# Attention and a quadratic ReLU FFN on one core: turned attention weights moved in one set of transfers for two head groups, and a planner with other costs, priorities and places

## The chip, the core and the metric

The kernel runs on one core of a Trainium2 chip. The metric is the device time of one execution in microseconds (us). TensorE (PE) multiplies, VectorE (DVE), ScalarE (ACT) and GpSimd (POOL) work on the results, and SyncE (SP) and GpSimd issue most of the transfers. TensorE has two clock levels, 1.2 and 2.4 GHz; the profile gives the granted clock as a share of the full one.

## What is computed

Attention runs inside chunks of 64 rows; its output, with the heads side by side, goes through a feed-forward network with a piecewise quadratic curve.

```python
# q, k, v: 8 x 8 x 576 x 64 (batch, heads, rows, head size), chunk = 64
scores = scale * np.matmul(q_c, k_c.transpose(0, 1, 2, 4, 3))
attn = np.exp(scores - max); attn = attn / (attn.sum(-1) + 1e-09)
out = np.matmul(attn, v_c)
x = out.transpose(0, 2, 1, 3).reshape(4608, 512)
h = x @ w_in                      # 512 x 2048
g = np.where(h >= 1, h, np.where(h <= -1, 0.0, (h + 1) ** 2 / 4))
y = g @ w_out                     # 2048 x 512
```

## The kernel before

**Tiles and groups.** The 4,608 tokens are 9 tiles of 512. A tile has 4 head groups of two heads each. The hidden width of 2,048 is 16 blocks of 128, so a tile has 16 steps of `ffn_in` (12 products of 512 columns) and 16 of `ffn_out` (12 products). Each number is carried as a high and a low part, hence three products for one.

**Stages.** Tiles 0 to 2 go step by step: `ffn_in(t, j)`, two steps later `ffn_out(t, j)`. Tiles 3 to 8 go in pairs (t, t+1). For a pair, `ffn_quad(t, m)` makes two hidden blocks of both tiles at a time with seven mixed products instead of eight (8 quads a pair). It finishes the blocks of tile t at once and sends those of tile t+1 to DRAM (`hold`). Then `recall(t+1, j)` reads them back, so that 16 steps of pure `ffn_out` follow. The mixed weights are made during tiles 1 and 2 by `mix_weights(m)` and written to DRAM (`to_mixed`), from where `load_mixed` reads them. The mixed inputs of a pair are made by `mix_x(t)` with 22 subtractions on VectorE and 14 casts on ScalarE.

**Attention between the steps.** From tile 2 on two head groups go together. `turn_next` transposes q and k of the next two groups into `qT` and `kT` (VectorE, L430). `burst` then makes the values of two groups and the scores of the next two on TensorE, the softmax (VectorE and ScalarE), and the turning back: VectorE transposes the weights in blocks of 32 x 32 into `qT` (L571), which is free by then, and transfers inside SBUF put the blocks in place in `aT` (L560). Behind that stand the loads of v for these groups and of q and k for the ones after them. Bursts stand at steps 4 and 10 of tile 1, at steps 0, 4, 8 and 12 of tile 2, and at quads 0, 2, 4 and 6 of the pairs 3 and 5 (`QUADS`). `turn_next` comes two steps before a burst, or just before the quad that the burst follows. The next `turn_next` writes q into the same `qT` buffers that the transfers of L560 read.

**Order.** Every operation is added to a `Plan` with an engine, a cost, and what it reads and writes. `Plan.emit` then simulates all engines and writes each engine's instructions in the simulated order. Among the parts that are ready on an engine, the one that was added first goes first. On the chip an engine takes its instructions in exactly this order. For a transfer the plan counts issuing (`cost`, split over `sends`), moving, and a `lag` until the data can be used:

```python
for _ in range(sends):
    end = max(end, landed[-self.UNDER_WAY]) + cost / sends
    moved = max(end, moved) + moving / sends
    landed.append(moved + lag)
```

The start order is written out: the loads of tile 0, then `load_more(6)` weights, q and k of tile 1, two more weights, v, four more weights.

Of the kernel before, what the change touches and what calls it, by code (L numbers as in the profile page):

```python
# [18 lines left out]
class Plan:  # L19
# [10 lines left out]
    def __init__(self):  # L30
        self.parts = []
        self.writer = {}
        self.readers = {}
        self.written = {}

    def add(
# [11 lines left out]
        for k in writes:  # L48
            self.written.setdefault(k, []).append(n)
        self.parts.append((engine, cost, emit, needs, lag, columns, port, moving, sends))  # L50
# [17 lines left out]
    def emit(self, filler):  # L68
# [32 lines left out]
        for _ in range(len(parts)):  # L101
            while True:
                best = None
                for e in engines:
                    while soon[e] and soon[e][0][0] <= free[e]:
                        heapq.heappush(now[e], heapq.heappop(soon[e])[1])
# [14 lines left out]
            while soon[e] and soon[e][0][0] <= start:  # L121
                heapq.heappush(now[e], heapq.heappop(soon[e])[1])
            n = heapq.heappop(now[e])
# [29 lines left out]
def kernel(  # L153
# [57 lines left out]
    qT_bufs, kT_bufs = buffers(sb, "qT", 2), buffers(sb, "kT", 2)  # L211
    e_bufs, aT_bufs = buffers(sb, "e", 1), buffers(sb, "aT", 2)
# [29 lines left out]
    words = {}  # L242
    weight = {}
# [40 lines left out]
    def load_weight(w, j):  # L284
# [12 lines left out]
        plan.add("sp", 0.57, emit, (), (f"{w}{j}_0", f"{w}{j}_1"), lag=2.1, moving=1.4)  # L297
# [95 lines left out]
    def load_heads(t, g, which="qkv"):  # L393
        for n, src, bufs in (("q", q, q_bufs), ("k", k, k_bufs), ("v", v, v_bufs)):
# [5 lines left out]
            if BATCH[t] is None or (n, t) == ("v", TURNED):  # L400
# [6 lines left out]
                (), (key,), lag=2.1, moving=1.3 if load == load_blocks else 1.2,  # L407
# [140 lines left out]
    def attn_turn_back(t, g):  # L548
# [3 lines left out]
        def move():  # L552


            src = x.rearrange("p (c e q) -> p c e q", e=2, q=Q)
            dst = aT.rearrange("p (c e q) -> p c e q", e=2, q=Q)
# [7 lines left out]
        if t < FLIPPED:  # L564
            pkey, ps = o_banks[1] if t == 0 else a_banks[0]
            plan.add("pe", 0.45, lambda: flip(ps, e), (ekey,), (pkey,), columns=T)
            plan.add("act", 0.48, lambda: nc.scalar.copy(out=aT, in_=ps), (pkey,), (akey,),
                     lag=late(t, 1.2))
        else:
# [163 lines left out]
    def mix_weights(m):  # L733
# [8 lines left out]
        def whole(n, dst):  # L742
            w = weight["wi", n].bitcast(F32)
            return nc.gpsimd.tensor_tensor(out=dst, in0=w[:, 0, :], in1=w[:, 1, :], op=ALU.add)

        def sum_of(out, x, y, op):
            return lambda: nc.gpsimd.tensor_tensor(out=out, in0=x, in1=y, op=op)
# [362 lines left out]
```

## Time and profile before

| | |
|---|---|
| Median of 3 runs (lowest, highest) | 858.1 us (855.43, 858.96) |
| The profiled execution | 859.44 us, span 857.7 us |
| PE busy | 827.9 us, 97% of the span |
| DVE busy | 554.5 us, 65% |
| ACT busy | 419.8 us, 49% |
| POOL busy | 202.4 us, 24% |
| Mean granted TensorE clock | 0.991 |

The span runs from the first to the last instruction on the engines. Busy TensorE time is a modelled figure, since products overlap; the waits of TensorE are a better measure of what is lost.

### The profile page before, as it was taken

The page shows a single profiled execution, that of the slowest core. Times are in us where ns is not written, and L with a number is a line of the kernel's source. Part 1 is how long each engine was busy: PE and PEld are TensorE (multiplying, and loading weights), DVE is VectorE, ACT ScalarE, POOL GpSimd, SP SyncE. Part 2 cuts the span into 40 slices and gives each one's busy share as a digit, 9 for nine tenths or more (in the row PEclk, how much of TensorE's full clock was granted, in tenths as well). Part 3 has the DMA queues.
Part 4 walks back from the last instruction along what each step waited for, and adds up shares of the span by engine and source line. Part 5 has one row for each costly group of instructions (what it writes and reads, how often), then busy time and mean ns, then how long its engine had stood idle before and what let it go on. Part 6 is the DMA issues. An engine that isn't in the chain of part 4 may idle for free.

```text
span 857.7 us, 15616 instructions
## 1 busy us (share of the span) xinstructions
PE 827.9 (97%) x5766; PEld 678.8 (79%) x5766; DVE 554.5 (65%) x921; ACT 419.8 (49%) x719; POOL 202.4 (24%) x326
## 2 busy tenths in 40 slices
PE   9799989999989999998999999899998999999998
PEld 8587867888878888786877888788886888888886
DVE  5788997757568778774769538577674255454422
ACT  5878864444445455443457224545563245444422
POOL 2221133365565201111112211211212112121210
PEclk9999999999999999999999999999999999999999
DMA  9878785663786656888697716975645254443432
GB/s 203 282 232 282 232 221 134 156 131 98 174 218 131 138 97 170 217 208 191 178 229 214 203 50 206 213 185 173 195 147 166 68 194 162 160 149 122 147 99 75
DMA packets 284828, 146.81 MB, mean 171 GB/s; under 512 B 249296, under 2 KB 257744, under 8 KB 284752
## 3 DMA queue, kind: packets, MB, share of 16 engines
q1 hardware_dynamic: 257728, 61.26, 32.5%
q0 software_dynamic: 24768, 83.90, 30.0%
q10 hardware_dynamic: 2256, 0.66, 0.4%
q8 instruction: 46, 0.75, 0.4%
q14 instruction: 30, 0.25, 0.1%
HBM read 101.71 MB, written 36.70 MB: 161 GB/s over the span
## 4 chain that ended last, share of the span: by engine, by line
PE 75%; DVE 6%; SPq 6%; DMA 5%; issue 5%; ACT 1%; POOL 1%; ACTq 0%; DVEq 0%; POOLq 0%
PE ps_o L670 38%; PE ps_h L847 20%; PE ps_h L635 12%; SPq L560 3%; PE ps_h L470 2%; PE ps_a L452 2%; DMA aT<-qT 2%; DMA words_wo<-in_moe_w_out_dram 1%; PE ps_a L670 1%; DMA q_sb<-in_q_dram 1%; SPq L387 1%; DMA k_sb<-in_k_dram 1%; DMA r<-held 1%; SPq L349 0%; DVE mx L526 0%
## 5 line engine op out<-in xcount | busy, mean ns | idle before, releaser
L670 PE MATMUL ps_o<-parts_wo,gh 128*128 128x512 f32 x1120 | 350.0, 394 | 3.8 <-DVE tmp L694 2.6
L670 PEld LDWEIGHTS ps_o<-parts_wo,gh 128*128 128x128 f32 x1120 | 209.4, 189 | 50.5 <-DVE tmp L694 4.1
L670 PE MATMUL ps_o<-parts_wo,gl 128*128 128x512 f32 x560 | 219.2, 391 | 1.2 <-DVE gl L656 1.2
L847 PE MATMUL ps_h<-big_wi,big_wi 128*128 128x512 f32 x720 | 174.8, 392 | 9.3 <-DVE big_wi L856 6.1
L847 PEld LDWEIGHTS ps_h<-big_wi,big_wi 128*128 128x128 f32 x720 | 135.1, 188 | 39.6 <-DVE big_wi L856 7.6
L656 DVE TENSOR_TENSOR gl<-r,gh 128x512 fp32r<-128x512 f32 x120 | 89.0, 742 | 72.1 <-ACT gh L655 68.0
L655 ACT CAST gh<-r 128x512 fp32r<-128x512 f32 x120 | 74.1, 618 | 119.5 <-PE ps_o L670 55.0
L635 PE MATMUL ps_h<-xh,parts_wi 128*128 128x512 f32 x376 | 125.1, 395 | 6.3 <-DVE r L646 3.7
L670 PEld LDWEIGHTS ps_o<-parts_wo,gl 128*128 128x128 f32 x560 | 105.7, 189 | 24.8 <-DVE gl L656 2.7
L778 POOL DMA_DIRECT2D big_wi<-mixed x84 | 45.1, 537 | 296.0 <-PE ps_h L847 288.7
L635 PEld LDWEIGHTS ps_h<-xh,parts_wi 128*128 128x128 f32 x376 | 70.6, 188 | 23.1 <-DVE r L646 4.6
L635 PE MATMUL ps_h<-xl,parts_wi 128*128 128x512 f32 x188 | 73.5, 391 | 0.0
L861 ACT ACTIVATE tmp<-big_wi 128x512 f32<-128x512 f32 x48 | 30.3, 632 | 73.1 <-DVE big_wi L856 65.8
L847 PE MATMUL ps_h<-xh,big_wi 128*128 128x512 f32 x192 | 63.3, 389 | 0.0
L642 ACT ACTIVATE r<-ps_h 128x512 f32<-128x512 f32 x47 | 27.8, 594 | 44.8 <-PE ps_h L635 44.5
L871 POOL DMA_DIRECT2D held<-tmp x48 | 26.5, 552 | 82.2 <-DVE tmp L865 76.3
L646 DVE SCALAR_TENSOR_TENSOR r<-ps_h,r 128x512 f32<-128x512 f32 x47 | 31.8, 677 | 19.8 <-ACT r L645 19.7
L430 DVE STREAM_TRANSPOSE qT<-q_sb 128x512 f32<-128x512 f32 x32 | 22.5, 705 | 33.3 <-DMA aT<-qT 20.8
L656 DVE TENSOR_TENSOR gl<-big_wi,gh 128x512 fp32r<-128x512 f32 x24 | 16.6, 690 | 40.2 <-ACT gh L655 40.1
L847 PEld LDWEIGHTS ps_h<-xh,big_wi 128*128 128x128 f32 x192 | 36.0, 188 | 7.5
L865 DVE SCALAR_TENSOR_TENSOR tmp<-big_wi,tmp 128x512 f32<-128x512 f32 x48 | 33.1, 690 | 13.5 <-ACT tmp L864 13.4
L635 PEld LDWEIGHTS ps_h<-xl,parts_wi 128*128 128x128 f32 x188 | 35.4, 189 | 7.1
(144 smaller groups left out, 1071.9 us busy)
## 6 DMA issues: line engine op xcount, KB each, us to landing
big_wi<-mixed POOLq DMA_DIRECT2D x84, 512.0 KB, 4.2
held<-tmp POOLq DMA_DIRECT2D x48, 256.0 KB, 3.9
words_wi<-in_moe_w_in_dram SPq DMA_DIRECT2D x16, 512.0 KB, 6.6
words_wo<-in_moe_w_out_dram SPq DMA_DIRECT2D x16, 512.0 KB, 8.2
out_dram<-tmp SPq DMA_DIRECT2D x31, 256.0 KB, 2.9
aT<-qT SPq DMA_DIRECT2D x224, 32.0 KB, 2.5
v_sb<-in_v_dram SPq DMA_DIRECT2D x52, 128.0 KB, 3.5
mixed<-parts_wi POOLq DMA_DIRECT2D x24, 256.0 KB, 3.8
```

The lines of the kernel that those rows point to most:

```text
L560: nc.sync.dma_start(out=dst[b:b + Q, :, i // 2, :], in_=src[a:a + Q, :, i % 2, :])
L635: nc.tensor.matmul(out=ps, lhsT=weight["wi", j][:, half, kc * P:(kc + 1) * P], rhs=x, start=(kc == 0 and i == 0), stop=(kc == KC - 1 and i ...
L642: plan.add("act", 0.48, lambda: nc.scalar.activation(out=r, in_=ps, func=AF.Relu, bias=0.5, scale=0.5), (pkey,), (rkey,))
L646: plan.add("dve", 0.6, lambda: nc.vector.scalar_tensor_tensor(out=r, in0=ps, scalar=1.0, in1=r, op0=ALU.max, op1=ALU.min), (pkey,), (rkey,))
L655: plan.add("act", 0.52, lambda: nc.scalar.copy(out=gh, in_=r), (rkey,), (ghkey,))
L656: plan.add("dve", 0.6, lambda: nc.vector.tensor_tensor(out=gl, in0=r, in1=gh.bitcast(F32), op=ALU.subtract), (rkey, ghkey), (glkey,), port ...
L670: nc.tensor.matmul(out=acc, lhsT=x[:, cols], rhs=weight["wo", j][:, half, :], start=(j == 0 and i == 0), stop=(j == NF - 1 and i == 2),)
L778: plan.add("pool", 0.65, lambda: nc.gpsimd.dma_start(out=place_of(f"wi{slot}").bitcast(F32), in_=mixed[u]), keys, (f"wi{slot}_0", f"wi{slo ...
L847: nc.tensor.matmul(out=bank, lhsT=w[:, c:c + P], rhs=x()[:, kc, :], start=start and kc == 0 and k == 0, stop=kc == 1 and k == 2, skip_grou ...
L861: plan.add("act", 0.5, lambda: nc.scalar.activation(out=r, in_=h(), func=AF.Relu, bias=0.5, scale=0.5), (hkey,), (rkey,))
L865: plan.add("dve", 0.6, lambda: nc.vector.scalar_tensor_tensor(out=r, in0=h(), scalar=1.0, in1=r, op0=ALU.max, op1=ALU.min), (hkey,), (rkey,))
L871: plan.add("pool", 0.65, lambda: nc.gpsimd.dma_start(out=held[j], in_=r), (rkey,), (f"held{j}",), lag=2.1, moving=0.8)
```

## The change

- One tile holds both `qT` buffers and one both `aT` buffers, side by side. `attn_turn_back_pair` transposes the weights of two groups and then moves both with one set of 8 transfers, each twice as large; before, each group had its own 8.
- The plan counts 5.4 us of issuing, 0.8 of moving and 4.9 of lag for that set, where it counted 4.8, 0.4 and 1.7 for a group. Loads of q, k and v for tile 3 and later get a lag of 4.1 instead of 2.1. The first six weight loads count 1.9 us of moving instead of 1.4.
- A part can be added with `plan.behind`: it is ranked as if it had been added that many parts later. `mix_x` is added so with 60 when it stands among the recalled steps.
- The six sums and differences of `mix_weights` run on VectorE instead of GpSimd, and the calls of `mix_weights` stand at other steps.
- Bursts of the pairs 3 and 5 stand at quads 0, 2 and 5 and at step 2 of the recalled tile, instead of quads 0, 2, 4 and 6.
- `load_more` at the start goes 4, 2, 6 instead of 6, 2, 4.

```diff
@@ Plan.add / Plan.emit
+        self.rank.append((n + self.behind, n))
...
-                        heapq.heappush(now[e], heapq.heappop(soon[e])[1])
+                        heapq.heappush(now[e], self.rank[heapq.heappop(soon[e])[1]])
...
-            n = heapq.heappop(now[e])
+            n = heapq.heappop(now[e])[1]
@@ buffers
-    qT_bufs, kT_bufs = buffers(sb, "qT", 2), buffers(sb, "kT", 2)
-    e_bufs, aT_bufs = buffers(sb, "e", 1), buffers(sb, "aT", 2)
+    qT_both, aT_both = (sb.tile([P, 2, T], F32, name=f"{n}_both") for n in ("qT", "aT"))
+    qT_bufs, aT_bufs = (
+        [(f"{n}{i}", both[:, i, :]) for i in range(2)] for n, both in (("qT", qT_both), ("aT", aT_both))
+    )
+    kT_bufs, e_bufs = buffers(sb, "kT", 2), buffers(sb, "e", 1)
@@ load_weight
-        plan.add("sp", 0.57, emit, (), (f"{w}{j}_0", f"{w}{j}_1"), lag=2.1, moving=1.4)
+        plan.add("sp", 0.57, emit, (), (f"{w}{j}_0", f"{w}{j}_1"), lag=2.1,
+                 moving=1.9 if len(asked) < 6 else 1.4)
+        asked.append((w, j))
@@ load_heads
-                (), (key,), lag=2.1, moving=1.3 if load == load_blocks else 1.2,
+                (), (key,), lag=2.1 if t < 3 else 4.1, moving=1.3 if load == load_blocks else 1.2,
@@ attn_turn_back (t >= FLIPPED), now attn_turn_back_pair
+        xkeys, akeys = ([f"{n}{i}" for i in range(2)] for n in ("qT", "aT"))
         def move():
-            src = x.rearrange("p (c e q) -> p c e q", e=2, q=Q)
-            dst = aT.rearrange("p (c e q) -> p c e q", e=2, q=Q)
+            src, dst = (x.rearrange("p g (c e q) -> p (g c) e q", e=2, q=Q) for x in (qT_both, aT_both))
             for j in range(2):
                 for i in range(4):
...
-            xkey, x = room("x", qT_bufs, t, g)
-            plan.add("dve", 0.6, lambda: nc.vector.transpose(out=x, in_=e), (ekey,), (xkey,))
-            plan.add("sp", 4.8, move, (xkey,), (akey,), lag=1.7, moving=0.4, sends=8)
+        for t, g in some:
+            ekey, e = e_room(t, g)
             xkey, x = room("x", qT_bufs, t, g)
+            plan.add("dve", 0.6, lambda x=x, e=e: nc.vector.transpose(out=x, in_=e), (ekey,), (xkey,))
+        plan.add("sp", 5.4, move, xkeys, akeys, lag=4.9, moving=0.8, sends=8)
@@ mix_weights
-            return nc.gpsimd.tensor_tensor(out=dst, in0=w[:, 0, :], in1=w[:, 1, :], op=ALU.add)
+            return nc.vector.tensor_tensor(out=dst, in0=w[:, 0, :], in1=w[:, 1, :], op=ALU.add)
...
-        plan.add("pool", 1.05, lambda: whole(i, a), keys[i], (akey,), port=True)
-        plan.add("pool", 0.6, sum_of(c[:, one], b[:, one], b[:, two], ALU.add), (bkey,), (ckey,), port=True)
+        plan.add("dve", 0.6, lambda: whole(i, a), keys[i], (akey,), port=True)
+        plan.add("dve", 0.35, sum_of(c[:, one], b[:, one], b[:, two], ALU.add), (bkey,), (ckey,), port=True)
...
@@ the order
-    load_more(6)
+    load_more(4)
     load_heads(1, 0, "qk")
     load_more(2)
     load_heads(1, 0, "v")
-    load_more(4)
+    load_more(6)
...
-    QUADS, LATE, MIX_X = (0, 2, 4, 6), -9, 3
-    MIX_AT = {18: (0,), 21: (1,), 24: (2,), 27: (3,), 30: (4,), 33: (5,), 36: (6,), 39: (7,)}
+    QUADS, LATE, MIX_X = (0, 2, 5), 2, 3
+    MIX_AT = {17: (0,), 21: (1,), 25: (2,), 29: (3,), 33: (4,), 37: (5,), 41: (6,), 45: (7,)}
...
-        for at in then:
-            attn_turn_back(*at)
+        if then:
+            attn_turn_back_pair(then)
...
             if j == MIX_X and t + 2 < NTILE:
+                plan.behind = 60
                 mix_x(t + 2)
+                plan.behind = 0
```

## Rows read from the trace of the kernel before

**Rows 1.** The waits of TensorE, asked for the stretches 0 to 60, 60 to 132, 132 to 324, 324 to 474, 474 to 646 and 646 to 858 us, in this order. Columns: who waited on which tile and line, for whom; us in total, times, the longest.

```profile
PE ps_h L635 <- DVE r L646: 3.4, 1, 3.4
...
PE ps_h L635 <- DVE parts_wi L332: 1.4, 2, 1.0
PE ps_o L670 <- DVE gl L656: 1.2, 1, 1.2
PE ps_h L635 <- ACT parts_wi L328: 1.2, 2, 0.9
PE ps_o L670 <- DVE parts_wo L332: 0.7, 1, 0.7
...
PE ps_h L470 <- DVE r L646: 2.2, 1, 2.2
...
PE ps_h L847 <- DVE big_wi L856: 6.1, 3, 3.0
PE ps_o L670 <- DVE tmp L694: 0.8, 1, 0.8
PE ps_h L847 <- DVE r L865: 0.7, 1, 0.7
...
PE ps_h L847 <- DVE r L865: 2.5, 1, 2.5
...
PE ps_o L670 <- DVE tmp L694: 1.8, 1, 1.8
```

**Rows 2.** First a piece of the chain that ended last (start, length, what), then two stretches of the table of stretches: length, busy time of PE, PEld, DVE, ACT and POOL with their instructions, the granted clock, the DMA share, GB/s.

```profile
474.27 35.36 PE ps_o L670 x156
...
398.00:401.20 3.20, 3.20 (x9) 2.46 (x10) 0.00 (x0) 0.00 (x0) 0.46 (x2) 0.56 0.94 277
38.00:43.20 5.20, 4.73 (x14) 3.80 (x15) 5.20 (x10) 4.32 (x8) 0.28 (x1) 0.69 0.73 219
```

**Rows 3.** SyncE's queue in order of time, at three bursts: the start of a run of issues, its length, what is issued, how many.

```profile
239.68 11.00 SPq L560 DMA_DIRECT2D aT<-qT  x16
...
349.36 11.79 SPq L560 DMA_DIRECT2D aT<-qT  x16
...
386.99 10.94 SPq L560 DMA_DIRECT2D aT<-qT  x16
```

**Rows 4.** VectorE in order of time, at the third of these bursts: start, length, instruction, and in brackets the idle time before it with what ended it.

```profile
395.37 0.71 DVE L430 STREAM_TRANSPOSE qT<-q_sb 128x512 f32<-128x512 f32 x1 [5.15 <-DMA aT<-qT]
...
401.88 0.71 DVE L430 STREAM_TRANSPOSE qT<-q_sb 128x512 f32<-128x512 f32 x1 [4.02 <-issue]
```

**Rows 5.** The same view at three other bursts.

```profile
249.81 0.71 DVE L430 STREAM_TRANSPOSE qT<-q_sb 128x512 f32<-128x512 f32 x1 [4.23 <-DMA aT<-qT]
...
358.32 0.71 DVE L430 STREAM_TRANSPOSE qT<-q_sb 128x512 f32<-128x512 f32 x1 [1.87 <-DMA aT<-qT]
...
548.50 0.71 DVE L430 STREAM_TRANSPOSE qT<-q_sb 128x512 f32<-128x512 f32 x1 [5.28 <-DMA q_sb<-in_q_dram]
```

**Rows 6.** First the issues of two lines (ns of one issue: least, median, most; first and last start), then the same transfers in the table of DMA issues (count, KB each, median us from issue to landing).

```profile
L560 SPq DMA_DIRECT2D aT<-qT x224: 585/609/1732, 139.5 to 608.3; - x112
...
L370 SPq DMA_DIRECT2D q_sb<-in_q_dram x96: 338/487/1594, 111.4 to 552.0; - x96
...
aT<-qT SPq DMA_DIRECT2D x224, 32.0 KB, 2.5
...
q_sb<-in_q_dram SPq DMA_DIRECT2D x96, 64.0 KB, 2.9
```

**Rows 7.** Around the turn from a pair's quads to its recalled tile: two pieces of the chain (a burst), VectorE in order of time (the first and the last instruction of a softmax with its turning, and two evictions), and the stretch of the recalled steps in the table of stretches.

```profile
410.60 0.88 PE ps_h L470 x55
...
411.53 0.95 PE ps_a L452 x56
...
446.95 1.29 DVE L526 TENSOR_REDUCE mx<-ps_a 128x8 f32<-128x512 f32 x2 [1.02 <-PE ps_a L452]
...
452.80 1.29 DVE L571 STREAM_TRANSPOSE qT<-kT 128x512 f32<-128x512 f32 x2
...
471.19 0.69 DVE L694 COPY tmp<-ps_o 128x512 f32<-128x512 f32 x1
...
474.00:510.00 36.00, 36.00 (x161) 29.81 (x160) 14.40 (x23) 8.63 (x14) 6.44 (x12) 1.00 0.52 127
...
647.10 0.69 DVE L694 COPY tmp<-ps_o 128x512 f32<-128x512 f32 x1 [1.58 <-DMA held<-tmp]
```

**Rows 8.** The sums of mixed weights on GpSimd (ns least, median, most), VectorE's group of half width (busy us, mean ns), a wait of GpSimd, and two VectorE instructions in order of time.

```profile
L744 POOL TENSOR_TENSOR e<-parts_wi x8: 1277/1290/1305, 117.5 to 270.4; 128x512 f32<-128x512 f32 x8
...
L619 DVE TENSOR_TENSOR xl<-ps_h,xh 128x256 fp32r<-128x256 f32 x2 | 0.8, 415 | 0.0
...
POOL e L744 <- DMA mixed<-e: 4.5, 4, 1.7
...
117.78 1.54 DVE L332 TENSOR_TENSOR parts_wi<-tmp,parts_wi 128x512 fp32r<-128x512 f32 x1
...
126.21 1.22 DVE L656 TENSOR_TENSOR gl<-r,gh 128x512 fp32r<-128x512 f32 x1
```

**Rows 9.** The start: SyncE's queue and VectorE in order of time.

```profile
23.51 11.14 SPq L362 DMA_DIRECT2D q_sb<-in_q_dram  x8
...
37.13 0.71 DVE L430 STREAM_TRANSPOSE qT<-q_sb 128x512 f32<-128x512 f32 x1 [1.65 <-DMA k_sb<-in_k_dram]
```

More of the change, by code (lines that the diff above doesn't have):

```diff
@@ L34, in __init__ @@
         self.written = {}
+        self.behind = 0
+        self.rank = []
     def add(
@@ L121, in emit @@
             while soon[e] and soon[e][0][0] <= start:
-                heapq.heappush(now[e], heapq.heappop(soon[e])[1])
-            n = heapq.heappop(now[e])
+                heapq.heappush(now[e], self.rank[heapq.heappop(soon[e])[1]])
+            n = heapq.heappop(now[e])[1]
             _, cost, emit, _, lag, columns, port, moving, sends = parts[n]
@@ L242 @@
     words = {}
+    asked = []
     weight = {}
@@ L550, in attn_turn_back, with attn_turn_back_pair @@
         akey, aT = room("aT", aT_bufs, t, g)
+        if t < FLIPPED:
+            pkey, ps = o_banks[1] if t == 0 else a_banks[0]
+            plan.add("pe", 0.45, lambda: flip(ps, e), (ekey,), (pkey,), columns=T)
+            plan.add("act", 0.48, lambda: nc.scalar.copy(out=aT, in_=ps), (pkey,), (akey,),
+                     lag=late(t, 1.2))
+    def attn_turn_back_pair(some):
+        xkeys, akeys = ([f"{n}{i}" for i in range(2)] for n in ("qT", "aT"))
         def move():
-            src = x.rearrange("p (c e q) -> p c e q", e=2, q=Q)
-            dst = aT.rearrange("p (c e q) -> p c e q", e=2, q=Q)
+            src, dst = (x.rearrange("p g (c e q) -> p (g c) e q", e=2, q=Q) for x in (qT_both, aT_both))
             for j in range(2):
@@ L743, in whole @@
             w = weight["wi", n].bitcast(F32)
-            return nc.gpsimd.tensor_tensor(out=dst, in0=w[:, 0, :], in1=w[:, 1, :], op=ALU.add)
+            return nc.vector.tensor_tensor(out=dst, in0=w[:, 0, :], in1=w[:, 1, :], op=ALU.add)
         def sum_of(out, x, y, op):
-            return lambda: nc.gpsimd.tensor_tensor(out=out, in0=x, in1=y, op=op)
+            return lambda: nc.vector.tensor_tensor(out=out, in0=x, in1=y, op=op)
         one, two = slice(0, HALF), slice(HALF, T)
-        plan.add("pool", 1.05, lambda: whole(i, a), keys[i], (akey,), port=True)
-        plan.add("pool", 1.05, lambda: whole(j, b), keys[j], (bkey,), port=True)
-        plan.add("pool", 0.6, sum_of(c[:, one], b[:, one], b[:, two], ALU.add), (bkey,), (ckey,), port=True)
-        plan.add("pool", 0.6, sum_of(c[:, two], c[:, one], a[:, one], ALU.subtract), (akey,), (ckey,), port=True)
-        plan.add("pool", 0.6, sum_of(b[:, one], a[:, one], b[:, one], ALU.subtract), (akey,), (bkey,), port=True)
-        plan.add("pool", 0.6, sum_of(b[:, two], a[:, two], c[:, two], ALU.subtract), (akey, ckey), (bkey,), port=True)
+        plan.add("dve", 0.6, lambda: whole(i, a), keys[i], (akey,), port=True)
+        plan.add("dve", 0.6, lambda: whole(j, b), keys[j], (bkey,), port=True)
+        plan.add("dve", 0.35, sum_of(c[:, one], b[:, one], b[:, two], ALU.add), (bkey,), (ckey,), port=True)
+        plan.add("dve", 0.35, sum_of(c[:, two], c[:, one], a[:, one], ALU.subtract), (akey,), (ckey,), port=True)
+        plan.add("dve", 0.35, sum_of(b[:, one], a[:, one], b[:, one], ALU.subtract), (akey,), (bkey,), port=True)
+        plan.add("dve", 0.35, sum_of(b[:, two], a[:, two], c[:, two], ALU.subtract), (akey, ckey), (bkey,), port=True)
         for skey, s_, which in ((ckey, c, (5, 6)), (bkey, b, (7, 3))):
```

6 lines of the change are left out of this document (removed).

## The prediction, made before the change was run

> **What bounds the kernel now.** I read the waits of TensorE first, stretch by stretch [rows 1], because TensorE's busy share says little here: its products are pipelined and overlap in the records. Where nothing waits, 156 products of 512 columns, 13 output steps of 12, follow each other in 35.36 us, 226.7 ns each, at the full clock (the first row of [rows 2]). A shorter time can therefore come only out of the waits, and out of the half-clock stretches behind the long ones. The rows of [rows 1] sum to 22.0 us in 15 waits, 1.47 us each. Behind the 3.0 us wait the granted clock was 0.56 of full speed for 3.2 us, behind the 3.4 us wait 0.69 for 5.2 us (the other rows of [rows 2]); at full being 2.4 GHz and half 1.2 GHz, these lose 3.2 x 0.44 = 1.4 us and 5.2 x 0.31 = 1.6 us. So 25 us is all that any reordering can return; the rest is work that the change leaves alone.
>
> Next I asked who is late. In the quad stages TensorE waits for a VectorE sum (L856) or curve (L865), but those are short; VectorE itself stood still before them. [rows 4] show it standing 5.15 us and then 4.02 us in front of a transposition of q (L430). What holds that instruction is in [rows 3]: the turned attention weights lie in the q buffers, and 16 transfers out of them occupy SyncE's queue from 386.99 for 10.94 us; the first q buffer came free at 395.37, the second at 401.88. The same instruction holds VectorE at three more places [rows 5]: 249.81 and 358.32 (behind the set that begins at 349.36), both for the transfer out of qT, and 548.50 for a load of q which stands on SyncE behind such a set. VectorE takes its instructions in the order that the planner wrote, so everything behind the transposition waits as well, the sums that TensorE needs among it.
>
> The planner put the transposition there because it believed the transfers quicker than they are. It counts 4.8 us of issuing, 0.05 of moving and 1.7 of lag: the first buffer free 6.55 us after the set begins. The trace has 395.37 - 386.99 = 8.4 us and 358.32 - 349.36 = 9.0 us. Two sets end for the planner after 4.8 + 6.55 = 11.35 us; the trace has 401.88 - 386.99 = 14.9 us, 3.5 us more, close to the 4.02 us that VectorE stood.
>
> **The change part by part.**
>
> One set for two groups. 28 sets of 8 become 14 of 8: 112 issues on SyncE go, each moved transfer carries 64 KB instead of 32 KB, and the bytes stay. An issue takes 0.609 us at 32 KB; loads of 64 KB (q, from DRAM) take 0.487 us and land in 2.9 us, where the 32 KB ones here land in 2.5 us [rows 6]. So bytes do not set the issue time of the nearest row. The lower bound for eight is 8 x 0.487 = 3.9 us; the present pitch is 10.94/16 = 0.68 us [rows 3], and if that goes with the bytes, eight take 10.9 us, the upper bound. I take the present pitch, 5.5 us, since the nearest row by place and kind is the transfer itself and the nearest by size is quicker still. From the eighth issue to the free buffer the trace shows 8.4 - 5.5 = 2.9 and 9.0 - 5.5 = 3.5 us. The merged set should free both buffers 8.4 to 9.0 us after its start, the first one no earlier than now, the second some 6 us earlier.
> The Trainium skill speaks of the same point: "DMA: Bandwidth & Descriptors", in the section on the anatomy of one DMA, counts about 2 us fixed for a transfer and only the moving by bytes, with descriptor generation small. By that rule the set costs no more issue time than half of today's pair, and the sum below stands; issue time in proportion to the bytes would give the first rival. The page's figures are for transfers issued by GpSimd, and no run here shows a 64 KB transfer inside SBUF.
>
> Slack in the plan. The new cost is 5.4 + 0.1 + 4.9 = 10.4 us until both buffers are free, 1.4 to 2.0 us more than I expect of the chip, so the planner now puts sums and curves ahead of the transposition. Loads for tile 3 and later count 2 us more, which covers the 548.50 case. This is worth the waits of the quad stages, 6.1 + 0.7 + 2.5 = 9.3 us [rows 1], and 1.4 us of half clock. Bounds 0 to 10.7; I take 9.0. The burst places (quads 0, 2, 5 and step 2 of the recalled tile) help the same waits: two of the three pairs get three quads or more between them instead of two. At 252.9 TensorE waited 2.2 us, with a set that needed 249.81 - 239.68 = 10.1 us; the new plan's 10.4 just covers that. Bounds 0 to 2.2; I take 1.5.
>
> The last burst of a stage moves into the recalled tile, where VectorE works 14.40 of 36 us [rows 7]. The mixing of x, which needs that burst, comes later with it, and gives way for 60 parts. Today it crowds the turn between tiles: the evictions (L694) at 471.19 and 647.10 are late and TensorE waits 0.8 and 1.8 us [rows 1, 7]. Gain up to 2.6. The price is a tight window: the products of the next quad begin at 509.6, three output steps of 12 x 0.2267 = 2.72 us stand ahead of the burst, which takes 0.88 + 0.95 = 1.8 us: 474.3 + 8.2 + 1.8 = 484.3, so VectorE has 25 us. It must do the softmax of two groups (446.95 to 454.1, 7.1 us), nine splits at 0.69 = 6.2 us, and of the mixing's 22 subtractions the 16 that hang on the last burst, 11.0 us: 24.3 us. It fits, barely; some of the operands are needed only later in the quad. Bounds: gain 2.6, loss 2 x 3.5 = 7.0 when none of the 22 is done early (28.5 us of work). I take a gain of 1.5.
>
> Sums of mixed weights on VectorE. GpSimd loses 48 instructions (1.29 us a whole one); VectorE gets 16 of 0.69 and 32 of 0.415 us, 24.3 us in all [rows 8], in tiles 1 and 2, where TensorE waited only once. What hides them is TensorE's lead of two steps over the splits. Against them: a sum can now stand at the head of VectorE while the transfer out of its buffer lands; GpSimd stood 4.5 us for that in 4 times [rows 8], and splits and curves are queued behind. Bounds 0 to 4.5 lost; I take 0.5. For them: at 117.78 and 126.21 a VectorE instruction of about 0.69 us took 1.54 and 1.22 us while GpSimd ran such a sum, and TensorE waited on both [rows 1, 8]. That is 0.85 + 0.53 = 1.4 us back; bounds 0 to 4.5 (all four waits between 60 and 132). I take 1.5.
>
> Load order at the start. Four weights instead of six stand before q and k of tile 1, whose eight q issues took 11.14 us and held VectorE until 37.13 [rows 9]. Two weights are 2 x 128 x 1,024 words, 1.05 MB; at 219 GB/s [rows 2] that is 4.8 us less ahead of q. The 3.4 us wait and its half clock (5.0 us) are the upper bound. On the other side two weights now stand behind 16 issues: if they come late, up to the same 5.0 us is lost. I take a gain of 1.5.
>
> A new order also makes waits of its own. I charge two of mean size, 2.9 us; the bounds are 0 and the 22 us of today.
>
> Sum: 9.0 + 1.5 + 1.5 - 0.5 + 1.5 + 1.5 - 2.9 = 11.6 us. The profiled execution took 859.4 (span 857.7): 847.8. The median of the runs, 858.1, lies 1.3 below it, so I forecast 847, with 841 to 853 as the range of this case.
>
> **The rivals.**
> *The merged set is slow.* If issuing goes with the bytes, both buffers come free after 10.9 + 2.9 to 3.5 = 13.8 to 14.4 us, 3.4 to 4 us beyond the plan, and VectorE stands at the transposition after every burst, as now. The 10.5 us of the quad stages and of 252.9 stay: 859.4 - 1.1 = 858.3, a median of 857. For it: the transfers inside SBUF are issued slower than the larger loads [rows 6]. Against it: those larger loads.
> *The waits only move.* The planner's costs are still estimates, and the new order may meet as many late arrivals as the old. With 10 us of new waits instead of 2.9 the median would be 854 to 857. For it: the 15 waits of today stand in a plan by the same rules; against it: most have one cause, which is dealt with.
> *Slower: the mixing comes late.* If the softmax and the splits go first and the mixing begins only when the next quad does, its 22 subtractions (15.2 us) hold the quads' products at the start of tiles 5 and 7. The other terms leave 11.6 - 1.5 = 10.1 us of gain, so from (10.1 + 4.3)/2 = 7.2 us at each place on the kernel is measurably slower; at 9 us each it takes 859.4 - 10.1 + 18 = 867, a median of 866. Against it: VectorE has 2 us free behind each split of that stretch (14.40 of 36), which the planner fills.
>
> **Chances.** Forecast 0.70, slow set 0.13, moved waits 0.09, late mixing 0.08. What a measurement can tell from no change here is about 0.5%, 4.3 us: 853.8 to 862.4. The forecast case is almost wholly faster, the slow set and nearly all of the moved waits are within, the late mixing is slower: 0.73, 0.19, 0.08. The range is 841 to 857; above it stay the late mixing and part of the two cases near 857.
>
> **What would show it.** Right: 112 transfers out of qT, pitch near 0.68 us; VectorE standing less than 1 us in front of a transposition of q; no TensorE wait over 1 us between 324 and 474 or 474 and 646; no half clock near 398. VectorE's instructions at 117 to 127 back to 0.69 us. Wrong: a pitch near 1.4 us; TensorE waiting for operands of the mixing (the splits that are L813 here) when a quad stage begins; a wait for prepared weights at 40 to 55 us; VectorE standing in front of a sum of weights for a landing transfer, with a split late behind it.

## The result, and the profile after it

The kernel after takes 834.3 us, the median of four runs (830.3 to 836.3), against 858.5 for the kernel before: a ratio of 0.971, 95% interval 0.965 to 0.976. It was measured once more, with six runs: 834.1 us, ratio 0.969 (0.965 to 0.973). The gain is 24 to 26 us; I forecast 11 from the median (847, range 841 to 857). The sign was right, the size less than half, and the time lies below the range.

The profiled execution after took 830.3 us (span 828.5), the quickest of its four, 4.0 below the median; before's profile, 859.4, is 0.9 above its own. So some 5 of the 29 us between the two profiles belong to these executions. The waits of TensorE in it, all that the view lists, to be read against [rows 1]. Columns: who waited on which tile and line, for whom; us in total, times, the longest. Line numbers are shifted by 9 to 15 (L648 is L635 of before, L683 is L670, L707 is L694).

```profile
PE ps_h L648 <- ACT parts_wi L337: 2.7, 1, 2.7
PE ps_o L683 <- DVE tmp L707: 1.5, 1, 1.5
PE ps_h L1085 <- POOL ident masks.py:199: 1.4, 1, 1.4
PE ps_h L648 <- DVE r L659: 0.7, 1, 0.7
PE ps_h L648 <- DVE parts_wi L341: 0.2, 1, 0.2
```

Of the 22.0 us of [rows 1] 5.1 are left beside the one at the very start (L1085). Every wait for the quads' sums and curves (L856, L865) is gone. The first row is new, at 41.9 us, and it is the wait for prepared weights at 40 to 55 us that the prediction named as a sign against it; the second is the turn back at 617, [rows 1]' last row, 0.3 us shorter.

SyncE's queue in order of time, in tile 2: start of a run of issues, its length, what, how many.

```profile
276.80 5.30 SPq L577 DMA_DIRECT2D aT_both<-qT_both  x8
282.20 4.29 SPq L379 DMA_DIRECT2D k_sb<-in_k_dram  x8
288.09 4.22 SPq L379 DMA_DIRECT2D q_sb<-in_q_dram  x8
292.40 3.63 SPq L396 DMA_DIRECT2D v_sb<-in_v_dram  x4
300.82 5.30 SPq L577 DMA_DIRECT2D aT_both<-qT_both  x8
```

And the issues of the merged set by themselves (ns of one issue: least, median, most; first and last start), with its landing:

```profile
L577 SPq DMA_DIRECT2D aT_both<-qT_both x112: 585/627/2735, 131.7 to 590.2; - x112
...
DMA to landing us min/median/max: 2.0/2.3/6.8
```

So 112 transfers, 627 ns where [rows 6] has 609 ns at half the bytes, 2.3 us to landing where it was 2.5. A set takes 5.3 to 8.4 us, its median is 5.4; those of before take 10.4 to 11.8. VectorE's waits for transfers, all of more than 0.5 us:

```profile
DVE e L757 <- DMA mixed<-e: 2.1, 1, 2.1
...
DVE tmp L707 <- DMA out_dram<-tmp: 1.6, 2, 1.4
DVE qT_both L439 <- DMA k_sb<-in_k_dram: 1.4, 2, 0.9
...
DVE tmp L757 <- DMA mixed<-tmp: 0.9, 1, 0.9
```

The transposition of q (L439, L430 of before) hardly waits for a turning transfer any more; in [rows 4, 5] single waits for one reached 5.15 us. The tile that the view names is not always the one waited for. In the traces the transfers of SyncE's queue signal the same eight semaphores in turn, and the view gives a wait to the last landing on any of them; the time at which each transfer lands tells them apart. By it the longer of the two waits named k, 0.9 us at 240.27, is for a set: its seventh transfer was issued at 235.64 and landed at 240.05. The first and the last of these rows are the head-of-line wait at a sum of weights that the prediction charged 0.5 us for: it came, 3.0 us in all, and no wait of TensorE follows it. VectorE at the place of [rows 8]' last two rows:

```profile
117.91 0.69 DVE L341 TENSOR_TENSOR parts_wo<-tmp,parts_wo 128x512 fp32r<-128x512 f32 x1
...
121.85 0.68 DVE L669 TENSOR_TENSOR gl<-r,gh 128x512 fp32r<-128x512 f32 x1
122.45 0.68 DVE L757 TENSOR_TENSOR e<-parts_wi 128x512 f32<-128x512 f32 x1
```

1.54 and 1.22 us have become 0.69 and 0.68, and the sum itself takes 0.68 where GpSimd needed 1.29. The table of stretches for the 36 us before the next quads, which begin at 483.2 (VectorE, the third of the busy times, works 25.34 of 36 us, with the burst's softmax in it, where [rows 7] have 14.40, and TensorE waits for nothing):

```profile
447.00:483.00 36.00, 36.00 (x161) 29.80 (x160) 25.34 (x44) 14.57 (x26) 5.37 (x10) 1.00 0.63 143
```

At the start, the eight q issues that took 11.14 us in [rows 9] take 6.86, from 21.21, and the first products of ffn_out begin at 34.5 us in place of 41.2.

**Where the time went.** For this I worked out TensorE's stops in each trace: every gap between the starts of two successive products that exceeds the product's own step by over 0.3 us, and beside it the clock lost, (1 - granted clock) times the length, in slices of 5 us from 20 to 825. The slices of before that are below full clock (length, busy PE, granted clock, DMA share, GB/s):

```profile
40.00:45.00 5.00, 5.00 (x17) 0.66 0.95 274
125.00:130.00 5.00, 3.02 (x17) 0.87 0.83 149
130.00:135.00 5.00, 5.00 (x107) 0.79 0.89 203
255.00:260.00 5.00, 4.62 (x131) 0.66 0.72 116
395.00:400.00 5.00, 2.08 (x6) 0.84 0.51 127
400.00:405.00 5.00, 4.30 (x16) 0.82 1.06 262
```

These are four episodes of 5 x 0.34 = 1.7 us each, 6.8 us. I had priced two of them, 3.0 us ([rows 2]). With the gaps, 28.3 us, before stops for 35.1 us, not for 25: a gap between two products is some 0.2 us longer than the wait that the view of waits lists for it, and the list of [rows 1] leaves out the wait of 1.2 us (a gap of 1.3) near 28 us. In after the gaps are 6.4 us and one episode is left.

| stretch, bounded by the first product of | before: length, stops | after: length, stops | gain | forecast |
|---|---|---|---|---|
| tile 0, to tile 1's ffn_in | 135.3, 15.2 | 126.1, 5.2 | 9.2 | 2.5 |
| tiles 1 and 2, to the first quad | 188.8, 4.6 | 184.2, 0.9 | 4.6 | 1.5 |
| pair 3's quads and recall, to tile 5's ffn_out | 199.8, 10.1 | 188.6, 0.0 | 11.2 | 10.5 with the next |
| the rest | 333.8, 5.3 | 329.6, 2.0 | 4.2 | |
| sum | 857.7, 35.1 | 828.5, 8.1 | 29.2 | 14.5, less 2.9 |

The rest of the span, 822.6 and 820.4 us, is the work itself, as the prediction said that it stays. The question for the experiments was which edit returned what, and by which cause.

### The profile page after: what moved, and what is told of

Its sections match the earlier page's. It is cut to its first block, busy times and chain, and to the rows that moved or that the text cites. A ratio compares the mean times of both kernels' runs of the same rounds, so it can differ in the third digit from the quotient of the medians.

```text
span 828.5 us, 15443 instructions
## 1 busy us (share of the span) xinstructions
PE 817.8 (99%) x5770; PEld 675.9 (82%) x5770; DVE 564.6 (68%) x969; ACT 421.9 (51%) x719; POOL 154.2 (19%) x278
## 5 line engine op out<-in xcount | busy, mean ns | idle before, releaser
L683 PE MATMUL ps_o<-parts_wo,gh 128*128 128x512 f32 x1120 | 347.8, 392 | 1.6 <-DVE tmp L707 1.5
L683 PEld LDWEIGHTS ps_o<-parts_wo,gh 128*128 128x128 f32 x1120 | 209.1, 188 | 46.4 <-DVE tmp L707 2.1
L683 PE MATMUL ps_o<-parts_wo,gl 128*128 128x512 f32 x560 | 218.2, 390 | 0.0
L860 PE MATMUL ps_h<-big_wi,big_wi 128*128 128x512 f32 x720 | 172.3, 389 | 0.0
L648 PE MATMUL ps_h<-xh,parts_wi 128*128 128x512 f32 x376 | 126.1, 396 | 3.6 <-ACT parts_wi L337 2.7
L669 DVE TENSOR_TENSOR gl<-r,gh 128x512 fp32r<-128x512 f32 x120 | 82.2, 685 | 63.9 <-ACT gh L668 63.2
L683 PEld LDWEIGHTS ps_o<-parts_wo,gl 128*128 128x128 f32 x560 | 105.2, 188 | 22.4 <-DVE gl L669 0.4
L648 PEld LDWEIGHTS ps_h<-xh,parts_wi 128*128 128x128 f32 x376 | 71.0, 189 | 19.8 <-ACT parts_wi L337 2.8
L648 PE MATMUL ps_h<-xl,parts_wi 128*128 128x512 f32 x188 | 73.7, 392 | 0.0
L874 ACT ACTIVATE tmp<-big_wi 128x512 f32<-128x512 f32 x48 | 30.3, 632 | 71.5 <-DVE big_wi L869 66.4
L869 DVE TENSOR_TENSOR big_wi<-ps_h,big_wi 128x512 f32<-128x512 f32 x48 | 32.9, 686 | 19.0 <-PE ps_h L860 13.8
L648 PEld LDWEIGHTS ps_h<-xl,parts_wi 128*128 128x128 f32 x188 | 35.6, 189 | 7.1
L741 POOL DMA_DIRECT2D mixed<-e x32 | 17.2, 542 | 125.5 <-ACT e L770 125.5
L669 DVE TENSOR_TENSOR gl<-big_wi,gh 128x512 fp32r<-128x512 f32 x24 | 16.6, 691 | 34.9 <-ACT gh L668 34.9
```

Source lines behind the costliest of these rows:

```text
L648: nc.tensor.matmul(out=ps, lhsT=weight["wi", j][:, half, kc * P:(kc + 1) * P], rhs=x, start=(kc == 0 and i == 0), stop=(kc == KC - 1 and i ...
L669: plan.add("dve", 0.6, lambda: nc.vector.tensor_tensor(out=gl, in0=r, in1=gh.bitcast(F32), op=ALU.subtract), (rkey, ghkey), (glkey,), port ...
L683: nc.tensor.matmul(out=acc, lhsT=x[:, cols], rhs=weight["wo", j][:, half, :], start=(j == 0 and i == 0), stop=(j == NF - 1 and i == 2),)
L741: nc.gpsimd.dma_start(out=dst, in_=src())
L860: nc.tensor.matmul(out=bank, lhsT=w[:, c:c + P], rhs=x()[:, kc, :], start=start and kc == 0 and k == 0, stop=kc == 1 and k == 2, skip_grou ...
L869: plan.add("dve", 0.6, lambda: nc.vector.tensor_tensor(out=out(), in0=bank, in1=x(), op=ALU.add), (key, xkey), (out_key,))
```

## The experiments

Each expectation was written before its run. In all of them theory A is the prediction's: VectorE stands in order at a transposition of q until a set of turning transfers has left the q buffers, and what TensorE needs stands behind it. Other letters are explained where they stand. Times are medians; the kernel before took 860.1 to 861.0 us beside these runs.

**Half of the set, nothing else.** In before, `for i in range(4)` of each set becomes `for i in (0, 3)`; the order on all engines stays, half of the turned weights stay away.

> The kernel before with only four of the eight transfers of each set issued (the other half of the turned weights is left out); the plan's costs and so the order of every engine stay as before. Theory A (VectorE standing at the transposition of q behind these transfers is what costs the waits of the quad stages and the one at 252.9): the first buffer is free about 2.7 + 3 = 6 us after the set begins, inside the plan's 6.55, so L430 no longer stands for aT<-qT, the waits for L856 and L865 in the quad stages go, and the time falls by 10 to 15 us, to 844 to 848. Tile 0 does not change. Rival B (the waits there come from the places of the bursts, which crowd VectorE): the time stays within 3 us of before.

Measured 844.6 us, ratio 0.982 (0.979 to 0.986): 15.6 us return with no other instruction moved. VectorE's wait for the set:

```profile
DVE qT L430 <- DMA aT<-qT: 2.5, 3, 1.4
```

And before, the same line of the view:

```profile
DVE qT L430 <- DMA aT<-qT: 20.8, 8, 5.1
```

By landing times it was 30.1 us in 10 waits there: the 4.02 us at 401.88 [rows 4] and the 5.28 us at 548.50 [rows 5] were for the set too. TensorE's stops in the quads of pair 3 fell from 10.1 to 0.9 us, in tiles 1 and 2 from 4.6 to 1.2. Theory A holds, and the burst places, which are the old ones here, did not cause those waits. The edit also takes 112 issues off SyncE's queue, so by itself it does not tell the wait for the q buffers from a wait for what is queued behind the set; the lines on VectorE's waits do.

**After's order, the set in its old pieces.**

```
-            for j in range(2):                      # 8 transfers of 64 KB
+            for g_, j in itertools.product(range(2), repeat=2):   # 16 of 32 KB
```

> The changed kernel with its plan and order as they are, but the set issued as 16 transfers of 32 KB instead of 8 of 64 KB. Theory A: the buffers come free some 14 to 15 us after the set begins instead of 8 to 9, past the plan's 10.4, VectorE stands 3 to 5 us in front of a transposition of q behind most bursts, and 8 to 14 us of the gain go: 842 to 848. Rival B: the lighter VectorE at the new places takes the wait up: 834 to 837.

Measured 851.5 us, 0.990 (0.987 to 0.993): 17 us lost, more than expected. VectorE's waits for transfers:

```profile
DVE qT_both L439 <- DMA aT_both<-qT_both: 9.7, 5, 4.4
DVE tmp L707 <- DMA out_dram<-tmp: 5.7, 2, 4.4
...
DVE qT_both L439 <- DMA k_sb<-in_k_dram: 4.6, 1, 4.6
DVE qT_both L439 <- DMA v_sb<-in_v_dram: 4.5, 1, 4.5
```

The view gives 9.7 us to the set, but the waits that it names k and v are for the set too. The one named v on VectorE, then SyncE's queue ahead of it:

```profile
396.27 0.71 DVE L439 STREAM_TRANSPOSE qT_both<-q_sb 128x512 f32<-128x512 f32 x1 [4.52 <-DMA v_sb<-in_v_dram]
```

```profile
382.80 8.68 SPq L577 DMA_DIRECT2D aT_both<-qT_both  x13
391.53 2.65 SPq L400 DMA_DIRECT2D v_sb<-in_v_dram  x4
```

This instruction reads q and writes where the set reads, and the set's last two transfers, issued at 390.20 and 390.85, landed at 395.97 and 396.15. The loads of v began only at 391.53, behind the set. The wait named k, at 540.77, ended with the set's last transfer in the same way (issued 534.31, landed 540.50). So 18.7 us in 7 waits are for the set, as theory A has it. One wait is of another kind: the store of out_dram was issued at 143.09, right behind a set that began at 132.30, and VectorE stood 4.4 us for it at L707. TensorE waited 3.3 us behind that, and the half clock after it lost 3.4. The prediction looked at the q buffers alone and had no such wait in it.

**Two sets, planned anew and honestly.** After, with `move(n_)` for each head group as in before, each with the long lag of 4.9.

> The kernel after with each head group's turned weights moved by a set of its own again (twice eight transfers, the planner told the same long lag of 4.9 us, everything planned anew). If the merging itself matters (SyncE issues 16 transfers in about 9.8 us in place of 8 in about 5): VectorE waits for the late set or for loads of k and v behind it, 842 to 852 us. Rival: an honest lag lets the planner put the transposition of q late enough, and the number of transfers is of no account, 834 to 838 us.

Measured 849.2 us, 0.987 (0.982 to 0.991): 15 us of after's gain are lost though the planner knows how long a set takes. SyncE's queue over one burst of tile 2, first in before, then here:

```profile
266.36 10.49 SPq L560 DMA_DIRECT2D aT<-qT  x16
276.95 2.14 SPq L370 DMA_DIRECT2D q_sb<-in_q_dram  x4
279.13 2.08 SPq L370 DMA_DIRECT2D k_sb<-in_k_dram  x4
281.31 2.03 SPq L370 DMA_DIRECT2D q_sb<-in_q_dram  x4
283.38 3.07 SPq L370 DMA_DIRECT2D k_sb<-in_k_dram  x4
286.55 2.27 SPq L387 DMA_DIRECT2D v_sb<-in_v_dram  x4
291.63 10.44 SPq L560 DMA_DIRECT2D aT<-qT  x16
```

```profile
258.96 10.54 SPq L577 DMA_DIRECT2D aT_both<-qT_both  x16
...
280.34 3.04 SPq L396 DMA_DIRECT2D v_sb<-in_v_dram  x4
285.90 10.71 SPq L577 DMA_DIRECT2D aT_both<-qT_both  x16
```

In before 22.1 of the 25.3 us from one set to the next are issuing; here the bursts come 26.9 us apart and the queue stops for 2.5 us; in after (the rows above) 17.4 of 24.0 us are issuing. The 9.6 us that this kernel loses in tiles 1 and 2, up to the first quad, go with stops of 9.9 us there, against 0.9 in after. The queue is not full even so: it pauses for 2.5 us from 283.38 and for 4.1 us from 308.92, each time until VectorE has turned the next weights. Only 1.5 us of VectorE's waits are for a set. TensorE's two longest stops behind tile 0 (waits of 2.5 us ending at 287.1 and 3.0 us ending at 384.3, both for a VectorE result, L660 and L870) stand behind a softmax on VectorE, and ahead of the first softmax VectorE stood 2.6 us, at 277.05, for a store of mixed weights that GpSimd issues. So the run prices the merging, 15 us with the lag held; by which path two sets cost that under this plan is not shown.

**Merging and slack alone.** Before plus the merged set and the new lags; loads, sums, burst places and ranking as before.

> The kernel before with the merged set and the slack in the plan alone (old start, old sums, old places, no rank behind). Theory A: what the halved set returned comes here too, 12 to 16 us: 843 to 847. Rival B: half of it or less, 851 or more, since VectorE is as crowded as before.

Measured 842.4 us, 0.979 (0.975 to 0.983): 17.7 us, above the 12 to 16 expected. TensorE's waits from 324 to 660 us, all of more than 0.4:

```profile
PE ps_o L683 <- DVE tmp L707: 2.1, 2, 1.8
```

Tile 1 starts at 135.1 us as in before, so nothing came out of tile 0; 4.1 us came out of tiles 1 and 2, 9.2 out of pair 3, 2.9 later.

**Merging without slack.** After, with `lag=1.7` for the set and `lag=2.1` for the loads.

> The changed kernel with the merged set, but the plan's lags as before: 1.7 instead of 4.9 us behind the set, 2.1 instead of 4.1 behind loads for tile 3 and later. Theory A: the plan then counts 5.4 + 0.1 + 1.7 = 7.2 us where the chip needs 8.4 to 9, so VectorE stands 1 to 2 us at the transposition behind most bursts; 2 to 7 us are lost, 836 to 841. Rival C (the shorter transfers are enough, the slack is not needed): 833 to 836.

Measured 841.5 us, 0.978 (0.974 to 0.982): 7 us lost, just above theory A's 836 to 841. C's figure did not come. VectorE's waits:

```profile
DVE qT_both L439 <- DMA k_sb<-in_k_dram: 9.0, 5, 4.6
DVE qT_both L439 <- DMA aT_both<-qT_both: 4.9, 3, 2.8
```

By landing times both lines are for the set: 13.5 us in 7 waits of 0.5 us and more, with the same 112 issues on the queue as in after. Between the first quads of the two pairs this profile takes 179.4 us instead of 172.9, so 6.5 us went there. So a planner that believes a transfer early puts the transposition too far ahead even when the set is short. Without the slack 7 us go, without the merging 15 (two_sets): neither replaces the other.

**Old burst places.** After with `QUADS, LATE = (0, 2, 4, 6), -9`.

> The changed kernel with the bursts of the pairs back at quads 0, 2, 4 and 6. Theory A: the transfers fit the plan at these places too, so at most 4 us are lost: 834 to 838. Rival B: the waits of the quad stages come back, 8 to 11 us: 842 to 846.

Measured 836.3 us, 0.975 (0.971 to 0.979): about 2 us lost, within the scatter (after's own interval is 0.965 to 0.976), and the two waits at the turn (L707, 2.1 us) are back. The rival that the places made the gain of the quads fell.

**No later rank for the mixing.** After with `plan.behind = 0`: the new places stay.

> The kernel after without the step that puts the mixing of a tile's inputs 60 places behind in the planner's ranking (the burst places stay new). By the theory that places and ranking only set VectorE's work at the turns between tiles: 0 to 2 us lost, 834 to 837 us, with a wait for tmp at a turn back. Rival: the mixing stands in front of the transposition of q at the new burst place after a tile's third quad, and a wait of 3 to 5 us per pair comes back: 838 us or more.

Measured 843.5 us, 0.980 (0.975 to 0.985): 9 us lost, where I expected at most 2. TensorE's waits, and the clock behind the first of them:

```profile
PE ps_h L860 <- ACT big_wi L824: 2.1, 1, 2.1
...
PE ps_h L860 <- DVE big_wi L826: 1.3, 1, 1.3
```

```profile
455.00:465.00 10.00, 6.64 (x27) 0.89 0.34 69
465.00:475.00 10.00, 9.74 (x34) 0.77 0.72 178
```

The two lines are the splits of the mixed inputs. TensorE's order has six products of the next quad ahead of output products that they follow in after; their operands come late, behind the softmax on VectorE. From the first quad to tile 5's ffn_out it takes 195.6 us instead of 188.6. The expectation's rival had the time, 838 or more, but not the cause: no transposition waits behind the mixing. It is the stop of the prediction's rival "the mixing comes late", TensorE waiting for operands of the mixing, here because those six products were ordered some 20 us ahead (462 instead of 483 us), with a price of 7.0 us at one turn (the prediction had it decide from 7.2 at each of two). It was in the new burst places, and the rank is what keeps it out. Without both, after would take some 835 us (merge_only's 842.4 less the 7 that start_and_sums gives: an estimate), so the places without the rank would have cost about 8. Another 4.2 us of this profile lie in tile 0, where both kernels issue the same instructions in the same order: there it is the execution.

**The start's load order.** First after with the old order (6, 2, 4 weights, moving 1.4), then before with the new one.

> The changed kernel with the weight loads of the start back at 6, 2, 4 and 1.4 us of moving for the first six. Theory A' (the 9 us gained in tile 0 are the start's: q and k of tile 1 ahead of two weights): the first ffn_out begins at 40 to 42 us again and 5 to 9 us are lost: 840 to 843. Rival B' (they are the sums', which no longer hold VectorE's and GpSimd's shared time): at most 2 us are lost.

> The kernel before with the new load order at the start and the larger moving cost of the first six weights alone. Theory A': 3 to 7 us are gained, all before tile 1 begins: 851 to 857, and the waits of the quad stages stay. Rival: below 2 us, since the gain in tile 0 needs the sums on VectorE as well.

After without it: 837.3 us, 0.974 (0.971 to 0.977), 3 us lost of the 5 to 9 expected, though tile 1 starts at 133.3 us instead of 126.1. Before with it: 857.7 us, 0.997 (0.994 to 1.001). There the first products of ffn_out begin at 34.7 us, 6.5 earlier than in before, and tile 1 at 133.7, only 1.6 earlier (its profile, 864.5, is 6.8 above its median): the time is given back near 42 us, and from 115 to 127, where TensorE waits 2.1 us for one split (gl) and 2.5 us in four other waits for prepared weights.

**The sums of mixed weights.** After with the sums on GpSimd and the old places; before with them on VectorE; before with both the loads and the sums.

> The changed kernel with the sums of mixed weights back on GpSimd at their old steps and costs. Theory A'' (after the run with the old start, which kept the waits at 116 to 125 us although the sums were on VectorE): the sums matter little, 0 to 2 us lost, 834 to 837. Rival D (GpSimd's sums hold VectorE in tiles 0 to 2): VectorE instructions of 1.2 us and more come back beside them and 3 to 6 us are lost.

> The kernel before with one part of the change alone: the sums for the mixed weights on VectorE at their new places, nothing else. Theory I (tile 0 gives its gain only when the early loads and the sums on VectorE come together, because either cause alone keeps tile 1's start at about 133 to 135 us): tile 1 starts at 132 to 135 us, the waits at the quad starts stay, 856 to 860 us. Rival J (the sums' waits at 115 to 127 us are a loss of their own, and taking them off GpSimd gives their price wherever the start stands): tile 1 starts about 5 us sooner, 853 to 855 us.

> The kernel before with the new load order and the sums on VectorE, and neither the merged set nor the slack nor the new burst places. Theory I (the two together free tile 0): tile 1 starts at 126 to 128 us as in the kernel after, the waits at the quad starts stay, 849 to 853 us. Rival K (the rest of the change is needed as well, since the planner re-orders tile 0 with every edit): tile 1 starts at 131 us or later, 855 us or more.

After without the sums on VectorE: 841.3 us, 0.978 (0.973 to 0.983), 7 us lost where I expected 0 to 2; the rival (D there) of 3 to 6 was nearer. A'' was my guess after the run with the old start, that the engine of the sums is of little account. GpSimd there, then VectorE at the same time:

```profile
117.97 1.29 POOL L757 TENSOR_TENSOR e<-parts_wi 128x512 f32<-128x512 f32 x1 [0.69 <-PE ps_a L423]
```

```profile
118.28 1.54 DVE L341 TENSOR_TENSOR parts_wo<-tmp,parts_wo 128x512 fp32r<-128x512 f32 x1
...
126.16 1.21 DVE L669 TENSOR_TENSOR gl<-r,gh 128x512 fp32r<-128x512 f32 x1
```

Tile 1 starts at 134.5 us, with one wait of 2.9 us for gl (L669) and 6.8 us of half clock in tile 0. Before with the sums alone: 857.6 us, 0.998 (0.994 to 1.001). With both: 852.9 us, 0.992 (0.989 to 0.995), about 7 us against 2.3 and 2.1. That is the time that theory I gave (the two free tile 0 only together; J: the sums pay by themselves; K: the rest is needed too), but its profile (857.6, 4.7 above the median) starts tile 1 at 131.1 us, K's figure, and not at 126 to 128. K's ground does not hold: up to 137 us every engine takes the same instructions in the same order as in after, so nothing else of the change is needed for that order. The intervals of the two alone reach 5 us; tile 1's starts, in the next run, say more on whether the two are worth more together than apart.

**Is tile 0's gain that of one execution?** After once more, unchanged.

> The kernel after, unchanged, once more on the chip of this call, with more executions. If the 7 to 9 us that tile 0 gave are a property of the order: tile 1 starts at 126 to 128 us in this profile too, and the median is 832 to 836 us. Rival (one fortunate execution, since five_first and start_and_sums showed 131 to 135 us in profiles well above their medians): tile 1 starts at 130 us or later and the median is 836 us or more.

Measured 834.1 us; tile 1 starts at 126.8. Until tile 1 starts, the kernels of this case have one of four orders in tile 0 (beside five_first's), and those of one row issue the same instructions in the same order:

| tile 0 has | tile 1 starts at, in the profile of each kernel | mean |
|---|---|---|
| neither edit | 133.6 half_set, 135.1 merge_only, 135.3 before | 134.7 |
| the load order | 133.7 start_only, 134.5 old_sums | 134.1 |
| the sums | 131.7 sums_only, 133.3 old_start | 132.5 |
| both | 126.1 after, 126.8 after_again, 127.0 split_set, 127.9 two_sets, 128.4 old_places, 130.3 no_behind, 130.6 no_slack, 131.1 start_and_sums | 128.5 |

So the order of after gives some 6 us there, and the execution decides how much: the 9.2 of the stops table is the upper end. The two edits gave 0.6 and 2.2 us apart and 6.1 together, more than their sum; with two profiles for each edit alone, this is likely and not settled.

**A fifth weight first.** After with 5, 1, 6 weights, an attempt to take away the new wait at 42 us.

> The kernel after with five feed-forward weight transfers in place of four ahead of the first loads of q and k (and one in place of two behind them). If TensorE's wait of 2.7 us near 42 us for the prepared weights, and the half clock behind it, come from the fifth weight's place in the queue: 830 to 833 us. If the later start of tile 1's first loads costs as much as it gives: 834 to 838 us, with a new wait for q or k in tile 0.

Measured 835.6 us, 0.970 (0.966 to 0.975), not told from after. The wait near 42 goes, others for prepared weights take its place, so the second expectation had the time, but not the cause: it named a wait for q or k.

```profile
PE ps_h L648 <- ACT parts_wi L337: 4.1, 2, 2.2
PE ps_o L683 <- ACT parts_wo L337: 1.4, 1, 1.4
```

These lie between 60 and 136 us, in a profile (841.4) that is 5.8 above the median. The q issues took 11.83 us again. No kernel here beats after.

Stops and spans of the profiled executions, worked out as above, show what every edit acts on: the span less the stops stays within 818 to 824 us. Read a row with its execution in mind: start_only's profile is 6.8 us and start_and_sums' 4.7 above the median.

| kernel | span | gaps | half clock | span less both |
|---|---|---|---|---|
| before | 857.7 | 28.3 | 6.8 | 822.6 |
| start_only | 862.7 | 30.3 | 10.2 | 822.2 |
| start_and_sums | 855.8 | 24.9 | 10.2 | 820.7 |
| two_sets | 845.5 | 20.0 | 1.7 | 823.8 |
| merge_only | 841.3 | 16.9 | 3.4 | 821.0 |
| old_sums | 839.4 | 13.5 | 6.8 | 819.1 |
| no_behind | 841.1 | 14.3 | 8.5 | 818.3 |
| after | 828.5 | 6.4 | 1.7 | 820.4 |

## Why the prediction was right and wrong

**Right: the cause, and the cost of the merged set.** The wait at the transposition of q behind the set was the main one (half_set, and by the landing times split_set and no_slack), and the set of eight took 5.4 us in the median, by the pitch of [rows 3], not 11; the two rivals that rested on a slow set and on waits that only move fell with it. The Trainium skill's "DMA: Bandwidth & Descriptors", in its section on the anatomy of one DMA, states a fixed cost for each transfer that GpSimd issues. These are issued by SyncE, and the rows agree in that neither figure grows with the bytes by much: 627 ns and 2.3 us at 64 KB against 609 ns and 2.5 us at 32 KB.

**Wrong: the bound of 25 us.** The sentence "So 25 us is all that any reordering can return" was read from the list of waits and two of four clock episodes. The trace held 35.1. Every term that was taken as a share of a listed wait was too small for the same reason; the wait at 252.9, for one, was bounded by 2.2 us and is a gap of 2.4 with 1.7 of half clock behind it, 4.1 us, and that is what merge_only returned in tiles 1 and 2 against my 1.5.

**Wrong: the quads and the wait at 252.9, 10.5 us.** merge_only measures the merged set and the slack at 17.7 (16.4 between the profiles). The mechanism was right and its size was not. The six stops of [rows 1] that these two terms name are gaps of 12.6 us with two episodes of half clock behind them, 3.4, so 16.0 us in before, and none of the six is left in merge_only. I bounded them by listed waits and one episode, 12.9 us, and took 10.5 of that. The causes were misread at one place: the 5.28 us at 548.50 were for the set and not for a load of q. The set's last transfer was issued at 541.64 and landed at 548.22, while the q that the view names was issued only from 542.35. So the longer lag of the loads covered nothing there; the set's own lag did. That something queued behind a set can cost time as well I did not ask; split_set's store at 143.09 is the one place where the runs show it.

**Wrong: the two values in tile 0.** Load order and sums were taken at 1.5 and 1.0 us net; before with both is 7 us faster. My bounds (5.0 and 4.5) held it; the thirds that I took of them had no row behind them. The sums' own price, 0.5, was right: nothing waits on them.

**Wrong in size, right in kind: the turn.** The window of 25 us was tight as computed: with the mixing ranked as before, the late mixing costs 7 us at one turn (no_behind). I gave the places and the rank one value, 1.5 us; they are two edits of opposite sign, about -8 us (estimated above) and +9.

**The charge of 2.9 us for new waits** did not fail: 2.9 and 0.3 us near 42 us, with 1.7 of half clock in one profile and none in the other, are what it was for. It was taken from a sum of 22.0 us that was itself 13 short of the stops.

By runs, 18 us for merging and slack (merge_only) and 7 for loads and sums (start_and_sums) make 25; places and rank together add what is left, within the scatter. What stays open is by which path two separate sets cost 15 us under an honest plan, how surely loads and sums are worth more together, and why the same instructions of tile 0 take 126 to 131 us.

## What to carry to other kernels

Where an in-order engine waits for transfers, find out which transfer really ended each wait: look at when those that the instruction depends on were issued and landed. The view names the last landing, and loads queued behind the set hid half of its cost (9.7 us listed, 18.7 by landing times). Then price the number of transfers and the plan's lags apart: with the same bytes, half the transfers were worth 15 us here and the longer lags 7. Price a stop as the gap between two products plus the clock behind it, not by its listed wait, and sum these over all of the trace before calling anything an upper bound. Two edits that belong together (a later burst and a lower rank for what hangs on it) get two values, the second of them without the first.

## What the hardware showed

The clock after a wait was not fixed. After and its repetition both stop for 2.9 us near 42 us, by the same instructions; the slice behind it, first in one and then in the other:

```profile
45.00:50.00 5.00, 4.85 (x14) 0.66 1.09 381
```

```profile
45.00:50.00 5.00, 4.19 (x17) 1.00 1.06 340
```

1.7 us in one, nothing in the other. The Trainium skill's "TensorE: Matmul & The Clock Gate", in its part on the clock gate, says that the number of slow products at the start of one kernel varies from run to run. The two rows show the like for a stop in the middle of a kernel, of which that passage does not speak.

VectorE beside GpSimd: a split of 0.69 us that began at 118.28, while GpSimd's sum ran from 117.97 to 119.26, ended at 119.82, 0.56 us behind the sum. The Trainium skill's "SBUF — State Buffer", in its section on the two separate sides, says that a VectorE instruction with two inputs in SBUF, as this split has, and a GpSimd one that reads SBUF lock each other out, and that the later of the two waits for the whole of the other. The row agrees to 0.13 us, since 119.26 + 0.69 would be 119.95.

Eight q issues at the start took 11.14 us behind six weights, 11.83 behind five and 6.86 behind four (before, five_first, after): not in step with the bytes ahead, and I have no run that explains the jump.
